# Seven products instead of eight in the first matrix product of three pairs of batches, and attention in stages of its own

## The chip, the cores and the metric

The kernel runs on one core of a Trainium2 chip. The metric is the time of the program on the device in microseconds, as the median of several runs. A core has a matrix engine (PE, with its weight loads shown as PEld), a vector engine (DVE), a scalar engine for activation functions (ACT), GpSimd (POOL, which here mostly issues DMAs) and a sync engine (SP, which here issues transposing DMAs and the stores). Matrix products land in PSUM, which has eight banks, each of 512 fp32 columns on 128 partitions.

## The reference

Eight batches, twelve heads, 448 positions, head size 64. Sigmoid attention is followed by a dense layer with silu.

```python
scores = q @ k.T / 8 - log(448)            # per batch and head
attn   = 1 / (1 + exp(-scores))
x      = attn @ v                          # 3584 tokens x 768
h      = x @ w_in                          # 768 -> 2048
g      = h * (1 / (1 + exp(-h)))
out    = g @ w_out                         # 2048 -> 768
```

## The kernel before

**Attention.** A group is four heads of one batch; there are 24 groups, three a batch. A group has seven tiles. `scores` makes four 64x64 matmuls for a tile, into the two banks of one PSUM tile `psc` (or into two single banks), and ACT turns the 896 columns into `attnT` with a sigmoid. When the seven tiles of a group are there, `values` makes 28 matmuls with `vf` into two banks `pav`, and DVE copies them, scaled by 64, into `xT` of the batch. k and q come in through POOL's queue (`kf`, `qf`, rings of four), are turned by PE for the first groups and later by a copy into `kr`, `qr` and a transposing DMA on SP's queue (`dma_transpose`) into `kT`, `qT`, rings of four as well.

**h.** `h_unit(b, fc)` makes one 128-row block of h of one batch: six matmuls of 448 columns into one bank `ph`, a sigmoid on ACT (`tsig`), and a product on DVE into `gTr`. A batch has 16 of them, so all eight batches take 768 matmuls.

**Out.** `out_set` takes two blocks of 128 tokens and computes their 768 output columns with seven products of eight matmuls instead of eight products, from sums of blocks of `gTr` (S, made on DVE for each set) and sums of blocks of `w_out` (T, made once by `w_sums`). Results go through `osb`, a ring of four, to the output by SP's queue. There are 14 sets.

**Order.** It is written out by hand. PE executes in the order of the program. The generator `all_moe` gives the steps of h and out: h of batch 0, h of batch 1, three sets, and so on; every second pair of batches has a fourth set, made of one block of this pair and one that was kept from the pair before (`kept`, copied on ACT). The main loop puts a burst of two or three tiles of attention on PE, then a `stretch` of steps from the generator, paced by the constants `paces`, `H_WEIGHT` and `SET_WEIGHT`. So attention for batches 2 to 7 lies among h and out steps alike. Sigmoids that would hold up ACT can be put off (`late_sigmoid`). Attention of the first two batches comes before and among h of batch 0.

**PSUM.** `ps_sc` has two tiles of two banks, `ps_1` four single banks, which `ph`, `pav`, `po` and the transposes share.

In the profile of before L196 is the score matmul, L207 and L180 the sigmoid of attention, L232 the value matmul, L243 the copy into xT, L262 the h matmul, L274 and L276 sigmoid and product of h, L338 the out matmul, L346 and L353 what follows it on DVE and ACT, L350 to L360 the sums S, L168 and L143 the copies ahead of the transposes, L169 the transposes, L308 the sums of w_out, L331 the stores.

Of the kernel before, what the change touches and what calls it, by code (L numbers as in the profile page):

```python
# [17 lines left out]
def kernel(  # L18
# [33 lines left out]
    p4 = ctx.enter_context(tc.tile_pool(name="p4", bufs=4))  # L52
# [14 lines left out]
    def new_flat(name, g):  # L67
        flat[name, g] = (p3 if name == "v" else p4).tile(
            [P, 2, NCH, D], F16, tag=f"{name}f", name=f"{name}f"
        )  # L70
# [62 lines left out]
    dummy = cpool.tile([P, 512], F16, tag="dummy", name="dummy")  # L133
# [30 lines left out]
    def dma_transpose(g, name, copy):  # L164
        if ("k", g) not in qkT:
            new_qkT(g)
        rows = p3.tile([P, NCH, 2, D], F16, tag=f"{name}r", name=f"{name}r")
# [7 lines left out]
    late = []  # L175

    def late_sigmoid():
        while late:
            to, psc = late.pop()
            nc.scalar.activation(to, psc, AF.Sigmoid, bias=bias_s, scale=QKSCALE)  # L180

    def scores(g, ch, banks=None, put_off=False):


        attnT[g, ch] = p12.tile([P, 2, S], F16, tag="attnT", name="attnT")
        if banks is None:
            psc = ps_sc.tile([P, 2, 512], F32, tag="pssc", name="psc")
            banks = [psc[:, j] for j in range(2)]
            parts = [(attnT[g, ch], psc[:, :, :S])]
        else:  # L190
            parts = [(attnT[g, ch][:, j], banks[j][:, :S]) for j in range(2)]
        for half in range(2):
            own = slice(half * HP, (half + 1) * HP)
            for j in range(2):
                rows = slice(j * D, (j + 1) * D)
                nc.tensor.matmul(  # L196
                    banks[j][own, :S],
# [5 lines left out]
        if put_off:  # L203
            late.extend(parts)
            return
        for to, psc in parts:
            nc.scalar.activation(to, psc, AF.Sigmoid, bias=bias_s, scale=QKSCALE)  # L207

    def single_banks():
        return [ps_1.tile([P, 512], F32, tag="ps1", name="psc1") for _ in range(2)]  # L210
# [36 lines left out]
    gTr = cpool.tile([P, NFC, 2 * S], F16, tag="gTr", name="gTr")  # L247
# [4 lines left out]
    hold = False  # L252
    weight = 1.0

    def h_unit(b, fc):
        nonlocal hold, weight
        weight = H_WEIGHT if b > 1 else 1.0
        hold = b > 1 and fc >= NFC - 2 or b == 1 and fc == NFC - 1
# [12 lines left out]
        if fc == NFC - 1:  # L271
            h_done.add(b)
        tsig = p3.tile([P, S], F16, tag="tsig", name="tsig")
        nc.scalar.activation(tsig, ph[:, :S], AF.Sigmoid, bias=0.0, scale=ISX)  # L274
        late_sigmoid()
        nc.vector.tensor_mul(  # L276
            gTr[:, fc, (b % 2) * S : (b % 2) * S + S], ph[:, :S], tsig
        )
# [3 lines left out]
    H_WEIGHT, SET_WEIGHT = 0.72, 1.28  # L282

    rows_of = out.rearrange("(b p c) e -> b c p e", b=B, c=NCH)

# [25 lines left out]
    kept = cpool.tile([P, NFC, P], F16, tag="kept", name="kept")  # L311

    def block(g):
        return gTr[:, :, g * P : (g + 1) * P]
# [4 lines left out]
    def out_set(a1, rows1, a2, rows2, last=False):  # L319
        nonlocal hold, weight  # L320
        weight = SET_WEIGHT
        lo, hi = slice(0, NHC), slice(NHC, NFC)
        osb = [p4.tile([P, DMODEL], F32, tag="osb", name="osb") for _ in range(2)]
        c11, c12 = (osb[0][:, nh * NO2 : (nh + 1) * NO2] for nh in range(2))
        c21, c22 = (osb[1][:, nh * NO2 : (nh + 1) * NO2] for nh in range(2))
        m1 = p2.tile([P, NO2], F32, tag="m1", name="m1")
# [18 lines left out]
        def plus(o, po, x, sign=ISX):  # L345
            nc.vector.scalar_tensor_tensor(  # L346
                out=o, in0=po, scalar=sign, in1=x, op0=ALU.mult, op1=ALU.add
            )
# [5 lines left out]
        late_sigmoid()  # L354
        nc.vector.tensor_sub(sg[1], sg[0], a1[:, lo])
        hold = False
        yield 163
# [132 lines left out]
    def after_transpose(g):  # L490
# [6 lines left out]
        elif g == 4:  # L497
            load("kq", 8)
# [146 lines left out]
```

## Time and profile before

| what | value |
|---|---|
| median of 3 runs | 378.34 us (378.03 to 378.56) |
| profiled execution: span from first to last instruction | 376.0 us |
| PE busy | 367.9 us, 98% |
| ACT busy | 243.2 us, 65% |
| DVE busy | 233.9 us, 62% |
| POOL busy | 66.1 us, 18% |
| h matmuls (L262) | 768 |
| out matmuls (L338) | 784 |
| granted clock of PE | 1.000 |

The page gives no total for the profiled execution besides its span; the span is 2.3 us under the median of the timed runs, and what lies around it is launch and end. The views used are: the busy times of engines over the span and in stretches of it; the chain of work that ended last, with the line of each piece; the groups of instructions with the mean time of one; the waits, with who ended them; and the timeline, where successive instructions of one kind stand in one row with the time of the first, how long they took together, and how many they were. An engine's idle time costs nothing when another engine sets the end. The busy time of PE is modelled at the ends of matmuls, so a row's length holds about 0.16 us beyond the time at which the next matmul could start.

### The profile page before, as it was taken

What the parts mean: (1) busy time and instruction counts of PE and PEld (TensorE: products, weight loads), DVE (VectorE), ACT (ScalarE), POOL (GpSimd) and SP (SyncE); (2) the same over time, 40 slices, a digit from 0 to 9 for tenths busy, and PEclk for the clock granted to TensorE, in tenths of its full rate; (3) what the DMA queues carried; (4) which work ended last, traced back from release to release, by engine and by line L of the source; (5) the groups of instructions that cost most, each with busy time, mean ns of one, the idle gap of its engine ahead of it and who ended that gap; (6) DMA issues with size and microseconds to landing.
All of it is one profiled execution on the core that took longest, in us unless ns stands there. A gap on an engine that the chain in (4) does not pass through costs nothing.

```text
span 376.0 us, 7623 instructions
## 1 busy us (share of the span) xinstructions
PE 367.9 (98%) x3081; PEld 189.2 (50%) x3081; DVE 233.9 (62%) x417; ACT 243.2 (65%) x355; POOL 66.1 (18%) x99
## 2 busy tenths in 40 slices
PE   7999999999999999999999999999999999999995
PEld 3554445555554455455555545544555445555663
DVE  2664447997666466548676547645675457556773
ACT  5998886778766866676557676677866685243000
POOL 8566432053211002102120200000010000000000
PEclk9999999999999999999999999999999999999999
DMA  8999999959999909909499834546072300200333
GB/s 131 200 204 201 205 203 204 180 89 142 215 178 182 217 2 111 189 32 118 71 160 161 145 92 75 51 108 75 0 149 36 85 2 2 54 30 2 83 86 84
DMA packets 65698, 42.79 MB, mean 114 GB/s; under 512 B 36096, under 2 KB 62208, under 8 KB 65664
## 3 DMA queue, kind: packets, MB, share of 16 engines
q0 software_dynamic: 27072, 22.58, 42.5%
q1 hardware_dynamic: 38240, 19.44, 29.0%
q8 instruction: 24, 0.39, 0.4%
q10 hardware_dynamic: 352, 0.30, 0.2%
q14 instruction: 10, 0.08, 0.1%
HBM read 45.61 MB, written 11.01 MB: 151 GB/s over the span
## 4 chain that ended last, share of the span: by engine, by line
PE 91%; DMA 3%; ACT 2%; POOL 2%; issue 1%; DVE 0%; POOLq 0%; ACTq 0%
PE ph L262 38%; PE po L338 34%; PE psc L196 9%; PE pav L232 8%; DMA qf<-in_q_dram 3%; ACT attnT L207 1%; POOL kf L82 1%; POOL vf L82 1%; PE ptrq L153 0%; POOL qf L82 0%; ACT tsig L274 0%; DVE gTr L276 0%; ACT attnT L180 0%; PE ptrk L153 0%; DVE osb L346 0%
## 5 line engine op out<-in xcount | busy, mean ns | idle before, releaser
L207 ACT ACTIVATE attnT<-psc,bias_s 128x896 f16<-128x896 f32 (+1 forms) x168 | 138.5, 894 | 45.1 <-PE psc L196 44.9
L262 PE MATMUL ph<-xT,w_in_sb 128*128 128x448 f16 x768 | 151.2, 353 | 0.0
L276 DVE TENSOR_TENSOR gTr<-ph,tsig 128x448 f16<-128x448 f32 x128 | 78.3, 623 | 71.4 <-ACT tsig L274 70.9
L262 PEld LDWEIGHTS <-w_in_sb 128*128 128x128 f16 x768 | 72.8, 98 | 74.0 <-issue 9.2
L274 ACT ACTIVATE tsig<-ph 128x448 f16<-128x448 f32 x128 | 68.3, 549 | 49.1 <-PE ph L262 48.2
L338 PEld LDWEIGHTS <-S 128*128 128x128 f16 x448 | 42.3, 98 | 33.5 <-issue 7.2
L346 DVE SCALAR_TENSOR_TENSOR osb<-po,osb 128x384 f32<-128x384 f32 x70 | 37.6, 554 | 22.2 <-PE po L338 21.9
L196 PE MATMUL psc<-qT,kT 64*64 64x448 f16 x672 | 49.1, 360 | 1.5 <-ACT qT L143 0.5
L243 DVE TENSOR_SCALAR xT<-pav 128x448 f16<-128x448 f32 x48 | 27.7, 620 | 28.9 <-PE pav L232 28.9
L82 POOL DMA_DIRECT2D vf<-in_v_dram x24 | 17.2, 718 | 161.0 <-PE pav L232 138.6
L338 PE MATMUL po<-T,S 128*128 128x384 f16 x224 | 40.6, 327 | 0.0
L338 PEld LDWEIGHTS <-gTr 128*128 128x128 f16 x304 | 28.7, 98 | 23.5 <-issue 5.4
L338 PE MATMUL po<-w_out_sb,S 128*128 128x384 f16 x224 | 39.9, 326 | 0.0
L232 PE MATMUL pav<-attnT,vf 64*64 64x448 f16 x672 | 38.1, 350 | 0.4 <-DVE gTr L276 0.4
L338 PE MATMUL po<-w_out_sb,gTr 128*128 128x384 f16 x192 | 34.9, 327 | 0.0
L196 PEld LDWEIGHTS <-kT 64*64 64x64 f16 x672 | 16.4, 105 | 28.3 <-issue 23.1
L232 PEld LDWEIGHTS <-vf 64*64 64x64 f16 x672 | 20.9, 107 | 12.6 <-issue 2.7
L346 DVE SCALAR_TENSOR_TENSOR osb<-po,m 128x384 f32<-128x384 f32 x42 | 23.2, 553 | 6.3 <-PE po L338 5.1
L180 ACT ACTIVATE attnT<-psc,bias_s 128x896 f16<-128x896 f32 x26 | 26.6, 1022 | 0.0
L353 ACT ACTIVATE m<-po 128x384 f32<-128x384 f32 x14 | 6.9, 495 | 23.7 <-PE po L338 23.7
L338 PE MATMUL po<-T,gTr 128*128 128x384 f16 x112 | 21.4, 326 | 0.0
L82 POOL DMA_DIRECT2D kf<-in_k_dram x25 | 18.0, 721 | 18.0 <-DVE kr L168 9.6
(43 smaller groups left out, 153.6 us busy)
## 6 DMA issues: line engine op xcount, KB each, us to landing
out_dram<-osb SPq DMA_DIRECT2D x54, 192.0 KB, 3.2
vf<-in_v_dram POOLq DMA_DIRECT2D x24, 224.0 KB, 6.1
kf<-in_k_dram POOLq DMA_DIRECT2D x23, 224.0 KB, 7.9
qf<-in_q_dram POOLq DMA_DIRECT2D x23, 224.0 KB, 8.1
w_in_sb<-in_moe_w_in_dram POOLq DMA_DIRECT2D x16, 192.0 KB, 8.3
w_out_sb<-in_moe_w_out_dram POOLq DMA_DIRECT2D x4, 768.0 KB, 15.7
kT<-kr SPq DMA_TRANSPOSE x18, 7.3
qT<-qr SPq DMA_TRANSPOSE x18, 6.7
```

The costliest lines, as they stand in the source:

```text
L82: nc.gpsimd.dma_start(flat[name, g][:, :, c0:c1].rearrange("p i c d -> p i (c d)"), rows_in(name, g)[:, :, c0 * D : c1 * D],)
L180: nc.scalar.activation(to, psc, AF.Sigmoid, bias=bias_s, scale=QKSCALE)
L196: nc.tensor.matmul(banks[j][own, :S], qkT["k", g][rows, ch, own], qkT["q", g][rows, :, own], start=True, stop=True,)
L207: nc.scalar.activation(to, psc, AF.Sigmoid, bias=bias_s, scale=QKSCALE)
L232: nc.tensor.matmul(pav[half][j * D : (j + 1) * D, :S], flat["v", g][own, j, ch, :], at[own, j, :], start=(ch == 0), stop=(ch == NCH - 1),)
L243: nc.vector.tensor_scalar_mul(xT[b][:, half * NQ + iq, :], pav[half][:, :S], SX)
L262: nc.tensor.matmul(ph[:, :S], w_in_sb[:, cc, fc * P : (fc + 1) * P], xT[b][:, cc, :], start=(at == 0), stop=(at == NCC - 1),)
L274: nc.scalar.activation(tsig, ph[:, :S], AF.Sigmoid, bias=0.0, scale=ISX)
L276: nc.vector.tensor_mul(gTr[:, fc, (b % 2) * S : (b % 2) * S + S], ph[:, :S], tsig)
L338: nc.tensor.matmul(po[:, :NO2], a[:, fc, :], w[:, fc, :], start=(fc == 0), stop=(fc == NHC - 1))
L346: nc.vector.scalar_tensor_tensor(out=o, in0=po, scalar=sign, in1=x, op0=ALU.mult, op1=ALU.add)
L353: nc.scalar.activation(m1, po, AF.Copy, scale=ISX)
```

## The change

- h of batches 0 and 1 stays as it was, but batch 1 takes silu in one pass of ACT instead of a sigmoid and a product on DVE.
- h of the other six batches is made in three pairs. `h_pair(m)` treats a pair of batches as the two column blocks and the two halves of w_in as the two row blocks of a 2x2 block product, and makes seven products of three matmuls for each of eight groups i. It uses sums of w_in (`w_in_sums`, SI1, SI2, SI4 and, in place, SI3) and sums of xT (`x_sums`, four subtractions, most of them in the out stage before, the last slice at the start of the h stage). Products m1 and m2 collect in a bank `pa`, m6 in a bank `pb`, and m7, m4 in bank c and m5, m3 in bank d of one two-bank tile `pcd` out of `ps_sc`. DVE makes five additions a group, two of them in place in PSUM; ACT copies m1 and makes four silu passes.
- Attention of a pair of batches now lies only in the out stage before the pair's h stage, 21 bursts of two tiles in each of three out stages. The h stages have none, except for the last round of values at their start. So ACT changes between sigmoid and silu at each border.
- `out_set` adds without a scale, since silu undoes the factor 64, and takes the products in another order, with seven additions on DVE and one copy on ACT.
- Rings of kf, qf, kT, qT and osb go from four to three, kr and qr from three to two, m1 from two to one; `kept` is now a part of `gTr`. Put-off sigmoids, single banks for scores and weights of steps are gone. Copies ahead of transposes stand on DVE, and in the h stages on POOL.

The core of the diff:

```diff
-            qkT[name, g] = p4.tile([P, NCH, P], F16, tag=f"{name}T", name=f"{name}T")
+            qkT[name, g] = p3.tile([P, NCH, P], F16, tag=f"{name}T", name=f"{name}T")
...
+        if b == 0:
+            tsig = room_x()[:, 0]
+            nc.scalar.activation(tsig, ph[:, :S], AF.Sigmoid, bias=0.0, scale=ISX)
+            nc.vector.scalar_tensor_tensor(
+                out=to, in0=ph[:, :S], scalar=ISX, in1=tsig, op0=ALU.mult, op1=ALU.mult
+            )
+        else:
+            nc.scalar.activation(to, ph[:, :S], AF.Silu, bias=0.0, scale=ISX)
...
+        sub(tx[m, 1][:, of], x1[0][:, of], x0[0][:, of])
+        sub(tx[m, 2][:, of], x1[1][:, of], tx[m, 1][:, of])
+        sub(x1[0][:, of], x1[1][:, of], x1[0][:, of])
+        sub(tx[m, 4][:, of], x0[1][:, of], tx[m, 2][:, of])
...
+        def m1(i):
+            bank[i, "a"] = ps_1.tile([P, 512], F32, tag="ps1", name="pa")[:, :S]
+            product(i, bank[i, "a"], wi[0][0], x0[:, :NQ])
+            got[i, 1] = scratch()
+            nc.scalar.activation(got[i, 1], bank[i, "a"], AF.Copy)
+        def m2(i):
+            product(i, bank[i, "a"], wi[0][1], x0[:, NQ:], start=False)
+            silu(i, 0, 0, bank[i, "a"])
+        def m6(i):
+            b = ps_1.tile([P, 512], F32, tag="ps1", name="pb")[:, :S]
+            product(i, b, si[2], tx[m, 2])
+            got[i, "u2"] = scratch()
+            plus(got[i, "u2"], b, got.pop((i, 1)))
+        def m5(i):
+            cd = ps_sc.tile([P, 2, 512], F32, tag="pssc", name="pcd")
+            bank[i, "c"], bank[i, "d"] = cd[:, 0, :S], cd[:, 1, :S]
+            product(i, bank[i, "d"], si[1], tx[m, 1])
+        def m7(i):
+            product(i, bank[i, "c"], si[3], x1[:, :NQ])
+            got[i, "u3"], got[i, 22] = scratch(), scratch()
+            plus(got[i, "u3"], bank[i, "c"], got[i, "u2"])
+        def h22(i):
+            plus(got[i, 22], bank[i, "d"], got.pop((i, "u3")))
+        def m4(i):
+            product(i, bank[i, "c"], wi[1][1], tx[m, 4], start=False)
+            plus(bank[i, "c"], bank[i, "c"], got[i, "u2"])
+            silu(i, 1, 0, bank[i, "c"])
+        def m3(i):
+            product(i, bank[i, "d"], si[4], x1[:, NQ:], start=False)
+            plus(bank[i, "d"], bank[i, "d"], got[i, "u2"])
+            silu(i, 0, 1, bank[i, "d"])
+        def silu22(i):
+            silu(i, 1, 1, got.pop((i, 22)))
...
+        order = [(m1, 0), (m1, 1), (x_sums, m, NQ - 1, NQ), (m2, 0), (m2, 1), (m6, 0), (m5, 0)]
+        order += [(m7, 0), (h22, 0), (m6, 1), (silu22, 0), (m5, 1), (m4, 0), (m3, 0)]
+        order += [(m7, 1), (h22, 1), (m1, 2), (silu22, 1), (m4, 1)]
+        for i in range(2, last):
+            order += [(m6, i), (m3, i - 1), (m5, i), (m7, i), (h22, i), (m2, i)]
+            order += [(m1, i + 1), (silu22, i), (m4, i)]
+        i = last
+        order += [(m6, i), (m5, i), (m7, i), (h22, i), (m3, i - 1), (silu22, i)]
+        order += [(m2, i), (m4, i), (m3, i)]
...
-        nc.vector.tensor_sub(sg[2], a1[:, lo], a2[:, lo])
-        nc.vector.tensor_add(sg[0], a2[:, lo], a2[:, hi])
+        add, sub = nc.vector.tensor_add, nc.vector.tensor_sub
+        add(sg[0], a2[:, lo], a2[:, hi])
         po = yield from product(a1[:, lo], wq[0][0])
-        nc.scalar.activation(m1, po, AF.Copy, scale=ISX)
-        late_sigmoid()
-        nc.vector.tensor_sub(sg[1], sg[0], a1[:, lo])
-        hold = False
+        nc.scalar.activation(m1, po, AF.Copy)
+        sub(sg[1], sg[0], a1[:, lo])
         yield 163
         po = yield from product(a1[:, hi], wq[1][0])
-        plus(c11, po, m1)
-        nc.vector.tensor_sub(sg[3], a1[:, hi], sg[1])
+        add(c11, po, m1)
+        sub(sg[2], a1[:, lo], a2[:, lo])
...
+        po = yield from product(sg[1], tw[2])
+        add(c12, po, m1)
+        sub(sg[3], a1[:, hi], sg[1])
+        yield 163
         po = yield from product(sg[2], tw[3])
-        plus(c22, po, m1)
-        yield 163
-        po = yield from product(sg[1], tw[2])
-        plus(c22, po, c22)
-        plus(c12, po, m1)
+        add(c22, po, c12)
...
+    for m in range(B // 2 - 1):
+        stream = sets(m)
+        dense = (3 + m % 2) * 7 * 8 * 163
+        bursts = NT_B
+        each = (dense - ENDING) / bursts + 500 + 1460 * 2 * NQ / bursts
+        done = due = 0.0
+        own = 2 * NQ * (m + 2)
+        for n in range(2 * NT_B * (m + 1), 2 * NT_B * (m + 2), 2):
+            spent = burst(n)
+            rows_if_any(own, nc.vector.tensor_copy)
+            stretch(stream, each / 2, spent)
+            rows_if_any(own, nc.vector.tensor_copy)
+            stretch(stream, each / 2)
+        for _ in stream:
+            pass
+        (g,) = waiting
+        values(g, NCH - 1)
+        stream = h_pair(m + 1)
+        next(stream)
+        next(stream)
+        waiting.clear()
+        values(g)
+        after_values(g)
+        for i, _ in enumerate(stream):
+            if i % 8 == 7:
+                rows_if_any(NQB, nc.gpsimd.tensor_copy)
+    for _ in sets(B // 2 - 1):
+        pass
```

More of the change, by code (lines that the diff above doesn't have):

```diff
@@ L173, with scores @@
     attnT = {}
[L175 to L182, printed above, removed]
-        attnT[g, ch] = p12.tile([P, 2, S], F16, tag="attnT", name="attnT")
[L186 to L191, printed above, removed]
+    def scores(g, ch):
+        attnT[g, ch] = p12.tile([P, 2, S], F16, tag="attnT", name="attnT")
+        psc = ps_sc.tile([P, 2, 512], F32, tag="pssc", name="psc")
         for half in range(2):
@@ L196, in scores @@
                 nc.tensor.matmul(
-                    banks[j][own, :S],
+                    psc[own, j, :S],
                     qkT["k", g][rows, ch, own],
@@ L202, in scores @@
                 )
[L203 to L210, printed above, removed]
+        nc.scalar.activation(attnT[g, ch], psc[:, :, :S], AF.Sigmoid, bias=bias_s, scale=QKSCALE)
     xT = {}
@@ L309, in w_sums, with block @@
                 yield
-    kept = cpool.tile([P, NFC, P], F16, tag="kept", name="kept")
-    def block(g):
-        return gTr[:, :, g * P : (g + 1) * P]
+    def block(m, g):
+        at = first_col(m) + g * P
+        return gTr[:, :, at : at + P]
     def row_blocks(m, g):
```

267 lines of the change are left out of this document (147 added, 120 removed).

## The prediction

> **What bounds the kernel now.** First the page: its busy table and the row of granted clock.
>
> ```profile
> span 376.0 us, 7623 instructions
> ...
> PE 367.9 (98%) x3081; PEld 189.2 (50%) x3081; DVE 233.9 (62%) x417; ACT 243.2 (65%) x355; POOL 66.1 (18%) x99
> ...
> PEclk9999999999999999999999999999999999999999
> ```
>
> PE is busy in 98% of the span at full clock. A busy PE can still be a stalled one, so next come the chain in order of time and the stretches.
>
> ```profile
> 56.50 18.84 PE ph L262 x99
> ...
> 344.58 27.31 PE po L338 x168
> ```
>
> ```profile
> 75.30:115.00 39.70, 39.69 (x367) 20.67 (x365) 29.73 (x57) 30.07 (x42) 12.38 (x18) 1.00 1.13 158
> ...
> 152.00:211.00 59.00, 59.00 (x498) 30.79 (x494) 37.79 (x69) 37.29 (x56) 8.51 (x12) 1.00 0.83 119
> ```
>
> An h matmul costs 18.84/99 = 0.190 us of PE, an out matmul 27.31/168 = 0.1625. From 75.3 us to 344.6 PE has next to no idle time, and after its first 1.5 us the view of waits knows no wait of PE over 0.5 us: time goes where PE's instructions go. The timeline of PE shows what one run of attention costs.
>
> ```profile
> 84.24 0.49 PE L338 MATMUL po<-w_out_sb,S 128*128 128x384 f16 x2
> 84.66 0.76 PE L196 MATMUL psc<-qT,kT 64*64 64x448 f16 x12
> 85.36 1.47 PE L338 MATMUL po<-w_out_sb,S 128*128 128x384 f16 x8
> ```
>
> Two out matmuls begin at 84.24, so the next could at 84.57; it begins at 85.36. The 12 score matmuls (three rounds of four, 0.19 us a round) thus cost 0.79 us, 0.22 over their rounds: the price of a change between 64x64 and 128x128 work. Last, the groups that give durations.
>
> ```profile
> L207 ACT ACTIVATE attnT<-psc,bias_s 128x896 f16<-128x896 f32 x116 | 111.2, 1012 | 18.4 <-PE psc L196 18.2
> L276 DVE TENSOR_TENSOR gTr<-ph,tsig 128x448 f16<-128x448 f32 x128 | 78.3, 623 | 71.4 <-ACT tsig L274 70.9
> L274 ACT ACTIVATE tsig<-ph 128x448 f16<-128x448 f32 x128 | 68.3, 549 | 49.1 <-PE ph L262 48.2 <-DVE T L308 0.6
> L481 ACT ACT_TABLE_LOAD x1 | 1.3, 1283 | 1.3 <-PEq L629 1.3
> ```
>
> The hand-overs, from the timeline of DVE and PE near the end: a product ends and the next starts at 353.52, the addition that reads it at 353.72, so PE to DVE is 0.20 us after the last issue.
>
> ```profile
> 353.52 2.76 PE L338 MATMUL po<-w_out_sb,gTr 128*128 128x384 f16 x16
> ```
>
> ```profile
> 353.72 0.56 DVE L346 SCALAR_TENSOR_TENSOR osb<-po,osb 128x384 f32<-128x384 f32 x1 [0.28 <-PE po L338]
> ```
>
> Likewise ACT to DVE 0.03 (a sigmoid of 58.35 + 0.54, a product at 58.92), DVE to DVE 0.03 (354.80 + 0.69 to 355.52), DVE or ACT to PE 0.06 (a DVE end at 47.43, PE at 47.49).
>
> **The change, part by part.**
>
> *Seven products.* Of six batches' 576 h matmuls 504 stay: 72 x 0.190 = **-13.7 us**, all on PE's path.
>
> *Attention only in out stages.* After 75.3 us the timeline has 51 runs of attention on PE (26 of three tiles, 24 of two, one of values alone). The new code makes 21 runs of two in each of three stages, and cuts the last values of a stage in two: 69 runs. 18 x 0.22 = **+4.0**.
>
> *The h stages alone.* Each of 8 groups i of a pair is seven products of 0.57 us, 3.99 us of PE; DVE has five additions (5 x 0.62 = 3.1) and ACT five passes (2.75), so by load PE would still bound. What decides is the waits. The banks c and d of a group are two halves of one PSUM tile (pcd), and the built program makes PE wait on the whole tile: the first matmul of m4 (into c) waits for h22 (which reads d), and that of m3 (into d) waits for the silu of c. So in the steady order m6 m3' m5 m7 m2 m1 m4 (m3' of the group before), from the end of m7: 0.20, u3 0.62, 0.03, h22 0.62, 0.06: m4 starts at 1.53 where PE is free at 1.14. Then m4 0.57, 0.20, the addition into c 0.62, 0.03, silu 0.55, 0.06: m3 starts at 3.56, where PE (after m6) is free at 2.67. Then m3, m5, m7: 1.71. One group takes 5.27 instead of 3.99, **1.28 more**. Additions are priced by the 128x448 row (623), the silu by the sigmoid row (549); neither an addition that writes PSUM in place nor a silu is in the trace. Bounds: additions 0.55 (the 128x384 row) to 0.69 (512 elements cast from PSUM, 683), silu 0.50 to 0.63 (the 128x448 sigmoids of L207, 631): group 5.0 to 5.6. I take the rows of the same shape.
>
> Now one stage from E, the end of the last out product. values and the two first m1 and m2 run to E+4.0. m6 needs the second sum of x (tx2): the last values are there at 2.97, two xT copies to 4.1, two additions of 448 f16 (0.38 each, estimated from 549 for 768 elements and 685 for 1024) to 4.84: 0.5 of stall. Groups 0 and 1 come in another order and lose 0.39 + 1.45 and 0.96 + 0.88; groups 2 to 5 lose 4 x 1.28; group 6 0.39; the last 0.39 + 2.12, because ACT's last five passes queue up before m3 may start. Together 12.2 a stage, **+36.6** for three (29 to 45 by the bounds).
>
> *Silu beside sigmoid.* Seven more table loads of 1.28. Those from sigmoid to silu lie behind the values and m1 (ACT has until the slot of a is needed, 5 us later). Those back to sigmoid are exposed: in-order ACT has the last silu, the load, then two sigmoids of 1.0, and the second scores of a stage need the last pcd, the fourth need the second sigmoid. After the first h stage: load done 2.0 us after PE's end, scores three and four wait to 3.1 and 4.0 instead of 2.2 and 2.4: 1.5. Before the four-set stage 1.65, before the second three-set stage 2.25, before the last (no attention) 0. **+5.4** (3, if the out matmuls cover more; 9, if later runs lag too).
> The load's row, 1283 ns, is followed by its activation at once. The Trainium skill (ScalarE: Activation LUTs, section What ACT_TABLE_LOAD costs) adds about 1380 ns of drain to each switch; by that the three exposed ones cost 4.1 us more and the sum would be 419. The only load in the trace came with nothing in front of it, so it can't show a drain.
>
> *Out sets.* One addition of S fewer before the first product, but S3 now comes behind c11 on DVE and feeds the fourth product: product two ends at 356.12 in the last stage, its addition ran 356.38 to 356.94, a 0.68 S behind it from 356.85 to 357.53; the fourth product is due at 357.42: 0.17 late, 4 times 0.7 in the last stage. In the ten others an attention run mostly covers it, but c11 also waits for m1, which queues on ACT behind two sigmoids; estimated 0.18 each. **+2.5** (0 to 5).
>
> *Rings and queues.* SP carries the same 36 transposes; between 82 and 112 us they landed 9 to 15.6 us after issue, stores 11.8 to 12.4. Transposes for groups 9 to 11 can now start only when the scores three groups back are done, some 13 us ahead of need, and osb of three lets a set's second tile wait for the store of the set before, about 9 us earlier. **+2.0** (0 to 6). POOL gains 12 copies (0.6 to 0.95 by the DVE and ACT rows of that copy): behind them are loads needed 20 us later, so 0. The first loads wait for slots freed at 7.4 us, when POOL gets to them at 8.3: 0. The sums of w_in (16 x 0.55) stand where DVE loses 16 products of 0.62: 0. The 8 kept copies on ACT (0.65) go, and six copies for transposes move from ACT to DVE (0.61); nothing waited for them: 0.
>
> **Sum.** -13.7 + 4.0 + 36.6 + 5.4 + 2.5 + 2.0 = +36.8: span 412.8. The median (378.34) lies 2.3 above the profiled span, launch and end around it, so **415 us**.
>
> **Rivals.**
> 1. *The waits on pcd cost nothing; PE still sets the pace, faster.* For it: loads of DVE (3.1) and ACT (2.75) fit in 3.99. Against it: the chain above is serial, and PE has two products for the one gap and one for the other. Price: h stages +1.5 instead of 36.6. With the other terms at their low ends -13.7 + 4.0 + 1.5 + 3 = -5.2: 373 us. It decides where a group loses under 0.28 us and the other terms stay low. The Trainium skill (PSUM — Partial Sum Buffer, Specifications (TRN2)) says that ScalarE and VectorE reach PSUM in parallel as long as they don't share a bank; by that the two banks need no wait on each other and this rival's time follows. No run here shows it, and the waits stand in the program all the same.
> 2. *The out stages become bound by attention too*: sigmoids (42 x 0.92 back to back, 38.6 of some 47 us) or late transposes stall each run. For it: the landings above. Against it: from 229 us on transposes landed in 3 to 5 us. Three waits of 3 us more and the upper ends of the table loads: 427 us.
> 3. *No seven products at all*: excluded, the built program has 504 matmuls of that line.
>
> **Chances.** Forecast 86%, rival 1 4%, rival 2 9%, near today's time 1%. Range from the bounds: lower ends -13.7 + 4 + 29.5 + 3 = +22.8 (401), upper ends +55 (433); not all ends come together: 402 to 428. Faster by over 0.2% (about what these runs can tell from no change) 0.04, within 0.01, slower 0.95.
>
> **What would show it.** Busy share of PE near 90% or less, with PE idle in three stretches of about 46 us; in the waits, PE pcd behind ACT gTr (some 0.9 us, about 7 a stage) and behind DVE part (0.4); a group every 5.2 to 5.3 us; eight table loads; out stages of about 50, 58, 50 and 37 us. Wrong it would be if a group takes near 4.0, or if PE stands in the out stages more than in the h stages.

## The result, and the profile after

The changed kernel takes **422.0 us** (median of 4 runs, 421.66 to 423.74) against 378.24 us for the kernel before beside it. The ratio is 1.117, with a 95% interval of 1.114 to 1.119. The forecast was 415 us in a range of 402 to 428, slower with a chance of 0.95. The profiled span grew from 376.0 to 419.9 us, where the sum of the prediction gave 412.8. Times below leave out a run that lies over 1.5% above the fastest run of the same kernel; this concerns one run with the smaller rings and one with the eighth product in the kernel with all edits.

In the profile of after, L328 is the matmul of the seven products, L338 the five additions of DVE, L322 the silu, L344 the copy of m1, L305 to L308 the sums of xT, L166 the copies ahead of the transposes, L180 and L187 scores and sigmoid of attention, L445 the out matmul, L459 and L460 the first result and the third sum of an out set. In kernels with one line more, L445 is L446. In rows of a timeline, the brackets hold the idle time of the engine ahead of the row and whom it waited for.

The page first: the busy line of the engines, PE's share in 40 slices of the span, and the clock that PE was granted.

```profile
span 419.9 us, 7584 instructions
...
PE 376.3 (90%) x3009; PEld 184.7 (44%) x3009; DVE 256.1 (61%) x445; ACT 255.2 (61%) x346; POOL 77.7 (18%) x111
...
PE   7999999899996888799999878879999978879995
...
PEclk9999999999999899899999999988999999999999
```

PE has 72 matmuls fewer and yet is busy longer, 376.3 us for 367.9, in a span that is longer still. One reason is the clock, which had no dip before and has some now: a mean of 0.980 over 419.9 us is worth some 17 us at half clock, by estimate, in which matmuls take twice as long. The row of PE has three dips, to values of 6 to 8, and they are the three h stages.

The same by stage, from the table of stretches (length, then busy time and number of instructions of PE, PEld, DVE, ACT and POOL, granted clock, DMA share, GB/s). The rows are, in turn, an out stage, an h stage, and so on.

```profile
75.40:124.70 49.30, 48.04 (x480) 23.99 (x479) 29.90 (x55) 42.84 (x47) 11.80 (x17) 1.00 0.99 140
124.70:173.90 49.20, 37.53 (x197) 17.35 (x196) 30.30 (x46) 21.54 (x40) 10.70 (x13) 0.97 0.76 78
173.90:232.70 58.80, 57.74 (x537) 27.93 (x540) 36.01 (x64) 43.70 (x48) 7.87 (x11) 0.97 0.72 108
232.70:281.10 48.40, 37.46 (x196) 17.26 (x196) 30.21 (x46) 21.68 (x40) 10.70 (x13) 0.96 0.51 78
281.10:332.90 51.80, 50.94 (x482) 24.67 (x484) 29.70 (x53) 43.06 (x47) 2.15 (x3) 0.94 0.39 72
332.90:378.20 45.30, 35.76 (x195) 16.81 (x196) 27.10 (x46) 21.67 (x40) 0.00 (x0) 1.00 0.07 18
```

Out stages take 49.3, 58.8 and 51.8 us, and the last one 37.5 (378.2 to the end of its matmuls at 415.7); forecast were 50, 58, 50 and 37. PE is busy there in 97% and more. The h stages take 49.2, 48.4 and 45.3 us with PE busy for 36 to 38, DVE for 27 to 30 and ACT for 22: nothing in them is full, so they are made of waits. The forecast for them was about 46 each, right for the third and short by 3.2 and 2.4 for the first two.

The view of waits says which (total, times, longest).

```profile
PE pcd L328 <- ACT gTr L322: 20.0, 21, 1.7
PE pcd L328 <- DVE part L338: 7.8, 23, 1.4
PE pb L328 <- DVE tx L306: 4.2, 3, 2.0
PE psc L180 <- ACT gTr L322: 1.9, 2, 1.1
PE psc L180 <- ACT attnT L187: 1.8, 3, 0.7
```

Waits are counted from the modelled end of the matmul before, which lies about 0.16 us behind the time at which the next could have started. The first two lines are thus 27.8 + 44 x 0.16 = 34.8 us of PE's time. One group of the steady part, from the chain of work in order of time (start, length, what):

```profile
153.34 1.88 PE pcd L328 x9
...
155.24 0.64 DVE part L338
...
155.90 0.64 DVE part L338
...
156.58 0.74 PE pcd L328 x3
...
157.35 0.64 DVE pcd L338
...
158.01 0.55 ACT gTr L322
...
158.61 1.88 PE pcd L328 x9
```

From m3 of one group to m3 of the next it is 158.61 - 153.34 = 5.27 us, the forecast to the hundredth. After m7 (the last of the nine) come two additions in a row and only then m4 (156.58), then an addition in place and a silu, and only then m3. PE is on this chain for 2.6 of 5.27 us. The first and last groups of a stage fit as well: in the third h stage all 16 waits of PE add up to 9.5 us, with 16 x 0.16 to 12.1, where the forecast was 12.2 a stage.

Two things were not foreseen. The first is at the start of an h stage; the timelines of DVE and of POOL there (start, length):

```profile
128.68 2.02 DVE L305 TENSOR_TENSOR tx<-xT 128x448 f16<-128x448 f16 x1
130.74 0.39 DVE L306 TENSOR_TENSOR tx<-xT,tx 128x448 f16<-128x448 f16 x1
131.05 1.12 DVE L307 TENSOR_TENSOR xT<-xT 128x448 f16<-128x448 f16 x1
```

```profile
128.64 0.94 POOL L166 COPY kr<-kf 128x896 f16<-128x896 f16 x1
129.52 0.93 POOL L166 COPY qr<-qf 128x896 f16<-128x896 f16 x1
...
131.82 1.12 POOL L166 COPY kr<-kf 128x896 f16<-128x896 f16 x1
```

Four subtractions of one shape: one takes 0.39 us, those whose time overlaps with a copy on POOL take 1.1 to 2.0. The one of 2.02 us starts 0.04 behind the first POOL copy and ends soon after the second. PE's pb matmuls wait for L306 behind it.

The second is the clock. The stretches around the third wait of that stage (length, PE busy, clock, DMA share, GB/s):

```profile
135.00:137.20 2.20, 0.73 (x4) 1.00 0.53 39
137.20:141.20 4.00, 3.75 (x12) 0.57 1.40 133
141.20:145.20 4.00, 3.27 (x18) 1.00 1.76 104
```

After a stretch in which PE worked for a third of the time, the granted clock fell to 0.5 (the 4 us shown hold a piece at full clock, so their mean is 0.57), and a product of three matmuls took 1.12 us where it takes 0.57. This happens four times, at the start and the end of each of the first two h stages.

In stretches of 0.1 us the four falls can be placed: they start at 137.41, 174.96, 239.81 and 280.77 us and last 3.41, 3.41, 3.41 and 6.83 us, and the times between their starts are 11, 19 and 12 times 3.413. Cut into stretches of that length on this grid, PE was busy for 0.94, 1.14, 1.42 and 1.45 us of the stretch ahead of each fall, and, from 33 us on, for 1.84 us or more of every stretch at full clock that no fall followed. The seven falls in four kernels of the experiments (c and d in two tiles, copies on DVE, the eighth product in the changed kernel, sigmoids for silus in the changed kernel) fit: PE was busy for 1.04 to 1.45 us ahead of each, and for 1.58 us or more where none followed. So in these traces the fall goes with PE's share in such a stretch, not with one long wait.

### The profile page after: what moved, and what is told of

Its sections match the earlier page's. It is cut to its first block, busy times and chain, and to the rows that moved or that the text cites. A ratio compares the mean times of both kernels' runs of the same rounds, so it can differ in the third digit from the quotient of the medians.

```text
span 419.9 us, 7584 instructions
## 1 busy us (share of the span) xinstructions
PE 376.3 (90%) x3009; PEld 184.7 (44%) x3009; DVE 256.1 (61%) x445; ACT 255.2 (61%) x346; POOL 77.7 (18%) x111
## 4 chain that ended last, share of the span: by engine, by line
PE 72%; DVE 14%; ACT 7%; issue 3%; DMA 2%; POOL 2%; DVEq 0%; ACTq 0%; POOLq 0%
PE po L445 32%; PE pcd L328 14%; PE psc L180 9%; PE pav L209 7%; DVE part L338 7%; PE ph L241 7%; ACT gTr L322 4%; DVE pcd L338 4%; DMA qf<-in_q_dram 2%; ACT attnT L187 2%; DVE xT L220 1%; DVE tx L305 1%; PE pa L328 1%; PE pb L328 1%; POOL kf L79 1%
## 5 line engine op out<-in xcount | busy, mean ns | idle before, releaser
L187 ACT ACTIVATE attnT<-psc,bias_s 128x896 f16<-128x896 f32 x168 | 159.3, 1008 | 26.6 <-PE psc L180 26.1
L322 ACT ACTIVATE gTr<-pcd 128x448 f16<-128x448 f32 x48 | 26.1, 544 | 54.7 <-DVE pcd L338 54.7
L180 PE MATMUL psc<-qT,kT 64*64 64x448 f16 x672 | 54.4, 370 | 4.6 <-ACT gTr L322 1.9
L445 PEld LDWEIGHTS <-S 128*128 128x128 f16 x448 | 41.1, 98 | 37.2 <-issue 10.5
L338 DVE TENSOR_TENSOR pcd<-pcd,part 128x448 f32<-128x448 f32 x48 | 30.3, 632 | 39.9 <-PE pcd L328 39.9
L220 DVE TENSOR_SCALAR xT<-pav 128x448 f16<-128x448 f32 x48 | 27.7, 620 | 34.8 <-PE pav L209 34.8
L328 PEld LDWEIGHTS <-w_in_sb 128*128 128x128 f16 x288 | 28.2, 99 | 40.1 <-issue 17.8
L445 PEld LDWEIGHTS <-gTr 128*128 128x128 f16 x336 | 31.9, 100 | 29.2 <-issue 11.5
L445 PE MATMUL po<-w_out_sb,gTr 128*128 128x384 f16 x224 | 44.1, 342 | 0.0
L445 PE MATMUL po<-T,S 128*128 128x384 f16 x224 | 43.0, 327 | 0.1
L328 PEld LDWEIGHTS <-SI 128*128 128x128 f16 x216 | 21.3, 98 | 48.8 <-issue 31.7
L445 PE MATMUL po<-w_out_sb,S 128*128 128x384 f16 x224 | 40.8, 327 | 0.0
L241 PE MATMUL ph<-xT,w_in_sb 128*128 128x448 f16 x192 | 38.7, 353 | 0.1
L328 PE MATMUL pcd<-xT,SI 128*128 128x448 f16 x72 | 18.2, 362 | 20.0 <-ACT gTr L322 20.0
L338 DVE TENSOR_TENSOR part<-pcd,part 128x448 f32<-128x448 f32 x48 | 30.0, 624 | 9.7 <-PE pcd L328 8.7
L180 PEld LDWEIGHTS <-kT 64*64 64x64 f16 x672 | 18.6, 104 | 35.6 <-issue 31.0
L328 PE MATMUL pa<-xT,w_in_sb 128*128 128x448 f16 x144 | 32.3, 358 | 0.1
L241 PEld LDWEIGHTS <-w_in_sb 128*128 128x128 f16 x192 | 17.8, 98 | 19.1 <-issue 3.7
```

Source lines behind the costliest of these rows:

```text
L180: nc.tensor.matmul(psc[own, j, :S], qkT["k", g][rows, ch, own], qkT["q", g][rows, :, own], start=True, stop=True,)
L187: nc.scalar.activation(attnT[g, ch], psc[:, :, :S], AF.Sigmoid, bias=bias_s, scale=QKSCALE)
L220: nc.vector.tensor_scalar_mul(xT[b][:, half * NQ + iq, :], pav[half][:, :S], SX)
L241: nc.tensor.matmul(ph[:, :S], w_in_sb[:, cc, fc * P : (fc + 1) * P], xT[b][:, cc, :], start=(at == 0), stop=(at == NCC - 1),)
L322: nc.scalar.activation(gTr[:, r * NG + i, col + c * S : col + (c + 1) * S], h, AF.Silu, bias=0.0, scale=ISX)
L328: nc.tensor.matmul(to, w[:, n, i * P : (i + 1) * P], x[:, n], start=(start and n == 0), skip_group_check=not start, stop=(n == NQ - 1),)
```

## Experiments

The theory: PE waits for a two-bank tile as a whole, and that is nearly all of the loss in the h stages; the rest is the slowed sums of x and the borders. The rivals: the group is bound by DVE's and ACT's work; the halved clock is what costs; the table loads are.

**c and d in two tiles.**

```diff
-            bank[i, "c"], bank[i, "d"] = cd[:, 0, :S], cd[:, 1, :S]
+            bank[i, "c"] = cd[:, 0, :S]
+            bank[i, "d"] = ps_1.tile([P, 512], F32, tag="ps1", name="pd")[:, :S]
```

> Edit: bank d of a group is a bank of its own out of ps_1; only bank c stays in a tile of ps_sc. Nothing is left out. Theory (PE waits on the whole two-bank tile, so m4 waits for h22 and m3 for the silu of c): the waits of PE pcd behind gTr (20.0 us) and behind the additions (7.8 us) go, a group takes 4.0 to 4.2 us instead of 5.26, each h stage shrinks by some 10 to 12 us, and the time falls from 422 to 384 to 391. Rival 1 (the group is bound by the work of DVE and ACT, not by the tile): a group stays at 5.0 or above and the time at 415 or above. Rival 2 (banks of ps_1 run short and a new wait on pa or pb takes its place): a group of 4.5 to 5.0, 395 to 410.

Measured: 387.0 us (1.022 of before, 1.021 to 1.024), 35.0 us less from one line. Its page, its waits and its timeline of PE:

```profile
PE 365.9 (95%) x3009; PEld 184.3 (48%) x3009; DVE 253.9 (66%) x445; ACT 254.1 (66%) x346; POOL 77.6 (20%) x111
```

```profile
PE pb L328 <- DVE tx L306: 4.2, 3, 2.0
...
PE pcd L328 <- DVE part L338: 1.0, 2, 0.7
```

```profile
149.78 0.73 PE L328 MATMUL pcd<-tx,w_in_sb 128*128 128x448 f16 x3
...
153.75 0.73 PE L328 MATMUL pcd<-tx,w_in_sb 128*128 128x448 f16 x3
```

From m4 to m4 it is now 3.97 us, seven products back to back. The waits on pcd behind gTr are gone, those behind the additions fell from 7.8 to 1.0. The additions, the copies and the silus are the same instructions on the same contents, and c and d lay in different banks before as well; what has changed is the tile that d belongs to, and with it whom PE waits for. Both rivals fall. The wait on pb (4.2) stays, since it has another cause.

**Copies on DVE instead of POOL.**

```diff
-                rows_if_any(NQB, nc.gpsimd.tensor_copy)
+                rows_if_any(NQB, nc.vector.tensor_copy)
```

> Edit: in the h stages the copies into kr and qr go from POOL to DVE. Nothing is left out. Theory (DVE's subtractions of two operands in SBUF, L305 to L308, are held up while POOL copies from SBUF): the subtraction of 448 f16 at the start of an h stage, 2.02 us in the first, takes some 0.4 us, PE's wait on pb falls from 1.8 to about 0.5, 1.3 us a stage, and the half clock that follows that wait in two stages goes too: 422 falls by 4 to 8 us, to 414 to 418. Rival (the subtraction is that slow by itself, or the wait has another cause): the subtraction stays above 1 us and the time at 422 give or take 1; by the copies of 0.6 us now in DVE's order it could even be 1 or 2 us more.

Measured: 417.7 us (415.25 to 418.31), 4.3 less than 422.0, at the near edge of what the theory gave. The profile is of the fastest run, in which the clock fell once (mean 0.994); the other three had 0.981 to 0.985 and took 2.3 to 3.1 us more, so the half clock, which the theory expected to go, mostly stayed. The timeline of DVE at the start of the first h stage:

```profile
129.10 0.38 DVE L305 TENSOR_TENSOR tx<-xT 128x448 f16<-128x448 f16 x1
129.51 0.39 DVE L306 TENSOR_TENSOR tx<-xT,tx 128x448 f16<-128x448 f16 x1
129.82 0.38 DVE L307 TENSOR_TENSOR xT<-xT 128x448 f16<-128x448 f16 x1
```

0.38 instead of 2.02 and 1.12 us, and PE's wait on pb falls from 4.2 to 0.9 us in all. So the subtractions were held up by POOL's copies, not slow by themselves. The Trainium skill (SBUF — State Buffer, section "SBUF: two separate sides") says that a VectorE operation with two inputs in SBUF and a GpSimd operation that reads SBUF take one pair of ports in turn, each for its whole instruction. The trace agrees for the subtraction of 2.02 us: it ends at 130.70, 0.25 us after the second POOL copy (130.45). An addition with one operand in PSUM (133.12), beside a POOL copy from 132.90, took its usual 0.61 us. The subtraction of 1.12 us started 0.77 us ahead of the third POOL copy, so its case is not cleared up by these times.

**Both edits.**

> Edit: both of the first two, c and d in banks of different tiles and the copies on DVE. Nothing is left out. Theory: the gains add up but for the clock dip that both remove: 379 to 386. Rival (with PE no longer waiting on the tile, the copies of 0.6 us in DVE's order delay the additions that PE needs, since DVE then has 3.1 us of additions in each 4.0): no better than the first edit alone, 385 to 392.

Measured: 381.6 us (1.0085 of before, 1.007 to 1.010), 5.4 less than with the first edit alone. The gains add up; DVE's copies in its own order, 0.6 us each, delay nothing that PE needs. The granted clock is 1.000.

**The clock by itself.** The waits stay, but PE gets something to do in the four longest waits of each h stage.

```diff
+        def hold(n):
+            pw = ps_1.tile([P, 512], F32, tag="ps1", name="pw")
+            for _ in range(n):
+                nc.tensor.matmul(pw[:, :S], w_in_sb[:, 0, :P], x0[:, 0], start=True, stop=True)
...
-        order = [(m1, 0), (m1, 1), (x_sums, m, NQ - 1, NQ), (m2, 0), (m2, 1), (m6, 0), (m5, 0)]
+        order = [(m1, 0), (m1, 1), (x_sums, m, NQ - 1, NQ), (m2, 0), (m2, 1), (hold, 9), (m6, 0), (m5, 0)]
-        order += [(m7, 0), (h22, 0), (m6, 1), (silu22, 0), (m5, 1), (m4, 0), (m3, 0)]
+        order += [(m7, 0), (h22, 0), (m6, 1), (silu22, 0), (m5, 1), (hold, 6), (m4, 0), (hold, 6), (m3, 0)]
...
-        order += [(m2, i), (m4, i), (m3, i)]
+        order += [(m2, i), (m4, i), (hold, 8), (m3, i)]
```

> Edit: the changed kernel with extra h matmuls of 0.19 us, whose result nobody reads, in PE's four longest waits of an h stage: 9 ahead of m6 of group 0, 6 ahead of its m4, 6 ahead of its m3, 8 ahead of the last m3. The waits themselves stay. Theory (PE's granted clock falls to 0.50 for some 4 us, twice after the start of an h stage and twice after its end, because PE stood for most of the 4 us before): the granted clock is 0.99 or more, the matmuls after the waits take 0.19 us again, and the time falls by 5 to 8 us from 422 to 414 to 417. Rival (the clock falls for another reason, such as the load of the whole chip at that moment): the dips stay, and the time is 421 to 425.

Measured: 420.7 us (420.29 to 420.88), 1.3 less. The mean clock is 1.00 and products after the waits take 0.57 us again, so idle time of PE is what halves the clock. But the price that was expected, 5 to 8 us, is not there: where PE ran at half clock, part of what it lost came off the wait that followed. The border at 175 us shows it: the 13 out matmuls behind the first scores take 2.29 us in place of 3.44, but then a wait of 0.30 us for a sigmoid comes up, and over the whole kernel the scores' waits for sigmoids grow from 1.8 to 2.8 us. Part of the gain may also have gone into matmuls that ran a little past the end of a wait.

**Where the gain of the seven products went.** An eighth product of three matmuls a group, whose result nobody reads, ahead of m3 in the changed kernel (three matmuls like those of `hold` above; in the kernel with all edits they write the unused second bank of c's tile):

> Edit: the changed kernel with an eighth product of three matmuls a group, 0.57 us, whose result nobody reads, ahead of m3 of each of the 24 groups. PE's work is again what it was without the seven products (72 x 0.190 = 13.7 us more). Theory (the gain of the seven products lies wholly inside the waits on the two-bank tile, since m3 waits 0.73 us in each group): a group stays at 5.26 to 5.35 us and the time at 420 to 424. Rival (the gain was on PE's path, as the term of -13.7 us in the sum has it): 433 to 437.

Measured: 419.6 us (419.16 to 420.51), not slower than without it but 2.4 us faster. Its waits:

```profile
PE pcd L328 <- ACT gTr L322: 7.7, 21, 1.0
PE pcd L328 <- DVE part L338: 7.2, 20, 1.4
```

The wait behind gTr fell from 20.0 to 7.7 us: most of the 24 x 0.57 = 13.7 us of matmuls went into it, and a group still takes 5.26 us (m3 at 153.91 and 159.17). The 2.4 us may come from the clock, 0.991 here for 0.980; this was not tested by itself. So in the changed kernel the 13.7 us that the seven products save do not shorten anything. The same eighth product in the kernel with all edits (below):

> Edit: the same eighth product of 0.57 us a group in the kernel with all edits together (375.6), ahead of m7 and into the unused second bank of the tile that holds c. Theory (with c and d apart PE is the bound of the h stages, at 4.0 us a group): a group takes 4.56 us and the time rises by 12 to 14 us to 387 to 390. Rival (DVE or ACT set the pace by now and hide it): by less than 5 us, below 381.

Measured: 387.3 us (385.48 to 390.79) for 375.6, so 11.7 us more for 13.7 us of matmuls, in two kernels whose runs spread by some 5 us each. The trace is sharper: a group takes 4.54 us (m4 at 149.23 and 153.77) for 3.97, so the 0.57 us of the product count in full in the steady groups.

**The table loads.** Every silu replaced by a sigmoid, so that ACT keeps one table, in the changed kernel and in the one with both edits.

> Edit: every silu is replaced by a sigmoid of the same shape, so g is the sigmoid of h and no longer h times it; the tables of ACT never change. Prices the table loads alone. Theory of the prediction (three exposed loads, 1.5, 1.65 and 2.25 us): 422 falls by 4 to 7 us to 415 to 418. Rival 1 (each switch also drains ACT for 1.38 us more): by 9 to 11 us, 411 to 413. Rival 2 (the loads lie beside out matmuls): less than 2 us, 420 to 422.

> Edit: the kernel with c and d apart and the copies on DVE (381.6), every silu replaced by a sigmoid of the same shape, so that g is not the kernel's g and the table of ACT never changes. Theory (in the changed kernel the load lay beside out matmuls that ran at half clock, which is why taking it away gave only 1.4 us; at full clock it shows in the scores' waits): 381.6 falls by 3 to 5 us to 376.5 to 378.5. Rival 1 (the borders are set by the last silus and the first sigmoids, and the load is a small part of it): by 0 to 2 us, 379.5 to 381.6. Rival 2 (each switch drains ACT for 1.38 us besides): by 6 us or more.

Measured: 420.6 us, 1.4 less, in the changed kernel, with runs between 419.5 and 423.1, which overlap with those of the changed kernel; 378.05 us (377.86 to 378.50), 3.5 less, in the other. First a border of the changed kernel in ACT's timeline (last silu, load, first two sigmoids):

```profile
174.86 0.54 ACT L322 ACTIVATE gTr<-pcd 128x448 f16<-128x448 f32 x1 [1.55 <-DVE pcd L338]
175.42 1.28 ACT L187 ACT_TABLE_LOAD   x1
176.72 1.91 ACT L187 ACTIVATE attnT<-psc,bias_s 128x896 f16<-128x896 f32 x2
```

Then PE's timeline behind the first h stage with both edits, and in the same place with one table:

```profile
161.97 2.29 PE L446 MATMUL po<-w_out_sb,gTr 128*128 128x384 f16 x13
164.41 0.38 PE L180 MATMUL psc<-qT,kT 64*64 64x448 f16 x4 [0.15 <-ACT attnT L187]
165.31 0.38 PE L180 MATMUL psc<-qT,kT 64*64 64x448 f16 x4 [0.51 <-ACT attnT L187]
```

```profile
160.41 2.29 PE L446 MATMUL po<-w_out_sb,gTr 128*128 128x384 f16 x13
162.63 0.57 PE L180 MATMUL psc<-qT,kT 64*64 64x448 f16 x8
```

At full clock, 13 out matmuls take 2.29 us, and the third and fourth scores then wait for the sigmoids that the load has put off. In the changed kernel the 13 matmuls of that border took 3.44 us, at half clock, and no score behind them waited. Only at the first border, at 75.4 us and full clock, did scores wait for the load there: 0.72 and 0.52 us, about the 1.4 us that were gained. The load is followed by its activation within 0.02 us, and starts within 0.02 us of the silu's end (174.86 + 0.54 = 175.40). The Trainium skill (ScalarE: Activation LUTs, section "What ACT_TABLE_LOAD costs") adds about 1.38 us of drain to a switch; by an estimate from that, three exposed switches would give 6 us or more. No run here shows such a drain.

**Out products first.** In the kernel with both edits, the first two out products of a stage come ahead of the first scores.

```diff
         own = 2 * NQ * (m + 2)
+        stretch(stream, 16 * 163)
```

> Edit: the kernel with c and d apart and the copies on DVE (381.6), and in each out stage with attention the first two out products (16 matmuls, 2.6 us) come before the first scores. They need only silus of the first batch of the pair. Theory (what is lost at the borders is PE's wait for the last silus of the stage, ACT's pass through them, the table load and the first two sigmoids, 7.3 us of PE in all three borders): the scores' waits there fall to 1 or 2 us in all and the time falls by 4 to 6 us, to 375 to 378. Rival (the wait moves to the second out product, which needs the silus of m4, or to the second burst of scores): less than 2 us, 380 to 382.

Measured: 377.6 us (375.85 to 380.53; 0.998 of before, 0.996 to 1.001), 4.0 less. The scores' waits for the silus (2.5 us) are gone and those for the sigmoids fell from 3.6 to 0.8, so more was lost at the borders than the table load. But a wait of another kind came up in the profiled execution, which took 379.7 us and was the second slowest of ten:

```profile
PE psc L180 <- DMA qT<-qr: 3.1, 2, 2.0
```

Transposes that had been in time now land late. PE is not early there: it would have reached the scores that waited 2.0 us at 109.8 us, where in the kernel without this edit it reached the same ones at 108.7. The two transposes into qT that scores waited for landed 17.1 and 13.9 us after they were issued, for 10.9 and 10.3 us in the kernel without this edit; what slows them was not tested. The runs of this kernel also spread more than those of the kernel without the edit (381.31 to 381.88).

**S3 ahead of c11.** In the kernel with both edits:

```diff
         sub(sg[1], sg[0], a1[:, lo])
+        sub(sg[2], a1[:, lo], a2[:, lo])
...
         add(c11, po, m1)
-        sub(sg[2], a1[:, lo], a2[:, lo])
```

> Edit: the kernel with c and d apart and the copies on DVE (381.6), and in out sets the sum S3 is made ahead of the addition into c11, not behind it. Theory of the prediction (out sets lose 2.5 us, most of it because S3 is late): 1.5 to 2.5 us less, 379 to 380. Rival (S3 is in time, as the waits of weight loads on S of 2.4 us in all say that lie beside PE's queue): within 0.5 us of 381.6.

Measured: 380.9 us (380.47 to 381.11), 0.7 less. Between the two: S3 was late, but by a quarter of what was forecast.

**All edits, and a better order of the h stage.** m5 of group 0 goes ahead of m6 (it needs an earlier sum of x), m3 of group 0 behind m7 of group 1, and the last group keeps the order of the others, which the two tiles now allow.

```diff
-        order = [(m1, 0), (m1, 1), (x_sums, m, NQ - 1, NQ), (m2, 0), (m2, 1), (m6, 0), (m5, 0)]
+        order = [(m1, 0), (m1, 1), (x_sums, m, NQ - 1, NQ), (m2, 0), (m2, 1), (m5, 0), (m6, 0)]
-        order += [(m7, 0), (h22, 0), (m6, 1), (silu22, 0), (m5, 1), (m4, 0), (m3, 0)]
-        order += [(m7, 1), (h22, 1), (m1, 2), (silu22, 1), (m4, 1)]
+        order += [(m7, 0), (h22, 0), (m6, 1), (silu22, 0), (m5, 1), (m4, 0)]
+        order += [(m7, 1), (h22, 1), (m3, 0), (m1, 2), (silu22, 1), (m4, 1)]
...
-        order += [(m6, i), (m5, i), (m7, i), (h22, i), (m3, i - 1), (silu22, i)]
-        order += [(m2, i), (m4, i), (m3, i)]
+        order += [(m6, i), (m3, i - 1), (m5, i), (m7, i), (h22, i), (m2, i)]
+        order += [(silu22, i), (m4, i), (m3, i)]
```

> Edit: c and d apart, copies on DVE, two out products before the first scores, S3 early, and in the h stages m5 of group 0 ahead of m6, m3 of group 0 behind m7 of group 1, and the last group in the order of the others. Theory (the seven products gain 13.7 us, the attention runs cost 4, and all the rest of the loss is waits that these edits remove): 381.6 less 4 to 6 at the borders, 1 to 2 for S3 and 2 to 3 in the h stages, so 371 to 376, faster than the kernel before at 378.4. Rival (ACT's tail at the border and the sums of x set the stage whatever PE does first): 378 to 381.

Measured: 375.6 us (372.94 to 377.42), 0.992 of before (0.989 to 0.995): faster than the kernel before, by 0.8%. In the profiled execution, a fast one of 373.5 us, what is left of PE's waits in the h stages and at the borders is small:

```profile
PE pcd L328 <- DVE part L338: 0.6, 2, 0.3
...
PE psc L180 <- ACT attnT L187: 0.5, 1, 0.5
```

**The rings.** The kernel before with osb at three, kr and qr at two, m1 at one.

```diff
-        osb = [p4.tile([P, DMODEL], F32, tag="osb", name="osb") for _ in range(2)]
+        osb = [p3.tile([P, DMODEL], F32, tag="osb", name="osb") for _ in range(2)]
...
-        rows = p3.tile([P, NCH, 2, D], F16, tag=f"{name}r", name=f"{name}r")
+        rows = p2.tile([P, NCH, 2, D], F16, tag=f"{name}r", name=f"{name}r")
...
-        m1 = p2.tile([P, NO2], F32, tag="m1", name="m1")
+        m1 = cpool.tile([P, NO2], F32, tag="m1", name="m1")
```

> Edit: the kernel before, with only some of its rings made smaller as the change has them: osb from four to three, kr and qr from three to two, m1 from two to one. kf, qf, kT and qT keep four, since the order of the kernel before asks for transposes four groups ahead. Theory of the prediction (rings and queues cost 2.0 us, of which osb and the copies ahead of transposes are a part): 0.5 to 2 us over the kernel before, 379 to 380.3. Rival (the stores and transposes land in time in rings of that size): within 0.3 us of it.

Measured: 383.2 us (382.43 to 387.20; 1.015, 1.012 to 1.019), 4.9 more than the kernel before: both the theory and the rival were too low. Two waits of this kernel, in ACT's and PE's timeline and in the view of waits:

```profile
72.05 0.95 ACT L143 ACTIVATE kr<-kf 128x896 f16<-128x896 f16 x1 [2.66 <-DMA kT<-kr]
...
74.98 1.29 PE L262 MATMUL ph<-xT,w_in_sb 128*128 128x448 f16 x6 [1.63 <-DVE gTr L276]
```

```profile
DVE osb L346 <- DMA out_dram<-osb: 3.9, 1, 3.9
```

With two of kr, ACT stands behind a copy until a transpose has read the slot, the sigmoids of h queue behind the copy, and PE stops for 1.6 us two engines further. The osb of three lets an addition wait 3.9 us for a store, and PE then waits 0.8 and 0.7 us for additions into osb. These three waits of PE come to 3.1 us, so part of the 4.9 stays open, and the rings were not tried one by one. In the changed kernel the copies stand on DVE and POOL, no addition into osb waits for a store, and copies wait for transposes on DVE (1.9 us in all) and POOL (8.6), where no wait of PE follows from it in the view; so this price is that of the kernel before, and what the rings cost the changed one was not measured. Rings of four for kT and qT were not tried in the changed kernel.

## Why the prediction was right, and where its terms were off

**The tile wait: right, to its size.** The term was +36.6 us, three times 12.2, of which 0.5 a stage was the wait on the sums of x; the rest is 35.1. Parting the tile gave 35.0, though this holds a little of the clock too (0.995 for 0.980). The group was forecast at 5.27 and takes 5.27; the two operations that the trace of before did not show came out at 0.632 us (addition in place, 0.623 taken) and 0.544 us (silu, 0.549 taken), so the rows of the same shape were the right ones. What carried the prediction was to write down whom each first matmul waits for, and not to compare loads: DVE and ACT are at 61% and the chain alone fixes the period.

**Seven products, -13.7: right only as half of a pair.** It was put on PE's path, and the 1.28 us of wait in a group are counted on top. The eighth product shows that the two must be taken together: in the changed kernel it costs nothing, with c and d apart 0.57 us a group and 11.7 us in all. A sum of both terms is right, either by itself would mislead.

**The sums of x, 0.5 a stage: mis-sized.** The estimate of 0.38 us for a subtraction was exact (0.38 with the copies away). The failed step is the price of 0 for POOL's copies: "behind them are loads needed 20 us later, so 0" looked at what queues behind them on POOL, and not at DVE, which they hold up. Taking them away gave 4.3 us in the changed kernel and 5.4 with the tile parted. The first two h stages, in which these copies run at the start, are the ones that were longer than forecast; the third has none and fits.

**Table loads, +5.4: mis-sized.** Eight loads came, as forecast. Taking them away gave 1.4 us in the changed kernel and 3.5 at full clock. The first border came as forecast: the h matmuls ahead of it let PE go at 75.26 us, and scores three and four start 3.1 and 4.0 us later. The step that failed is the cover in the other two, put at 1.65 and 2.25 us: the out matmuls there ran at half clock and no score waited for the load. PE's wait for the last silus, 1.9 us in two borders, is there with one table as with two. The lower bound (3) was the better value.

**Out sets, +2.5: mis-sized**, 0.7 for the part that was tried. The prediction charged every set; the out stages of the changed kernel, 97% and more busy, leave little to charge.

**Rings, +2.0: open.** 4.9 us in the kernel before, in part by the mechanism named (osb and stores), and in part by one that was not (a copy in ACT's order that waits for a transpose). In the changed kernel no PE wait shows it.

**Attention runs, +4.0:** not tested by itself. The out stages have the lengths that it gave to within 1.8 us.

**The rivals.** Rival 1 asked for a group that loses under 0.28 us; it is true of the kernel with the tile parted, and then -13.7 is not enough either: 387.0, and 381.6 without POOL's copies. Only with the borders and the order mended is it faster than before, 375.6, 2.6 above the 373 that the rival gave. What the Trainium skill (PSUM — Partial Sum Buffer, section Specifications (TRN2)) says of ScalarE and VectorE at different banks was no ground for this rival: it bears on the banks, and PE's waits came from the tile in the program. Rival 2, bound out stages, did not come.

**The sum** was 7.1 us under the span of 419.9. By stages, the first two h stages and the out stages behind them are 8.2 us longer than forecast, and the rest 0.9 shorter; these are the stages with POOL's copies and with the half clock. Taking the copies away gave 4.3 us, and keeping the clock up gave 1.3. But loads (5.4 for 1.4) and out sets (2.5 for 0.7) were too high by some 4 to 6 us, so about as much more was missed, and no run shows what it is; the parts do not simply add, since the half clock and the loads hide each other at the borders. That the time came out only 7 us above the forecast is therefore in part luck: terms too high stood against costs that were not seen. The tile wait, which gives the sign and most of the size, is not luck.

## What to carry to other kernels

Before a product count is lowered, write down for the first matmul of each product which engine must have let go of its tile, tile and not bank, and add up that chain for one period: if it is longer than PE's work, the saved products buy nothing. Two accumulators whose readers come at different times belong in two tiles. A copy put on POOL because POOL is idle can be paid for by an operation of DVE beside it whose two operands both lie in the on-chip memory, as the subtractions did here, so look at who else reads that memory at that moment, and not only at POOL's queue.

## What was not expected of the hardware

- A subtraction of 448 f16 on DVE takes 0.38 us, and 1.1 to 2.0 us while POOL copies 896 f16 (0.93 to 1.12 us each).
- PE's clock fell to 0.5, for 3.41 us or twice that, although no wait of PE was longer than 2.0 us: ahead of each fall PE was busy for 1.45 us or less of 3.41. In the third h stage, with waits of 0.4, 0.2, 1.3 and 0.8 us at its start and one of 1.7 us at its end, it stayed at 1.00. With matmuls in the waits it stayed at 1.00 throughout. Keeping it up gave only 1.3 us here.
- A table load of 1.28 us had no gap ahead of it or behind it above 0.02 us.
